# Forward product of a row block as one 512-column operand instead of two of 258, in a re-planned order

## The chip, the cores and the metric

The kernel runs on one core of a Trainium2 chip. The metric is the device time of one execution in microseconds (us); smaller is better. A profiled execution gives, beside it, the span from the first to the last instruction and what each engine did in it: PE (matrix products; PEld is its weight load), DVE and ACT (element-wise work, and copies between the matmul's result memory PSUM and the working memory SBUF), POOL and SP (here both used to issue DMA transfers).

## The reference

Two branches of the same size are mixed by a gate per row. Branch A filters its input in the frequency domain, branch B is a two-layer perceptron with GELU:

```python
# x, w_r, w_i: A_x (1, 2048, 512), (2048, 257); b: w1 (512, 1792), w2 (1792, 512)
X = rfft2(x)                       # over rows and columns
a = irfft2(X * (w_r + 1j * w_i), s=(2048, 512))
h = gelu(x @ w1 + b1)
b = h @ w2 + b2                    # both branches read A_x
g = sigmoid((x * gate_w).sum(-1))
out = g * a + (1 - g) * b
```

All of it is float32. The kernel keeps that precision by splitting each operand of a product into a high and a low part in a 12-bit-mantissa form (fp32r) and taking three matmuls, high times high, high times low and low times high.

## The kernel before

**Staging.** The 2048 rows are 16 residue classes j of 128 rows each (names like `xr4` or `py5` carry j). Five kinds of work share PE, and its results are named in the profile: `pd` and `py` are the forward transform of A, `pz` and `pa` its inverse, `ph` and `po` the two layers of B. The forward work of all blocks lies between about 10 and 120 us, and B's first half runs in between it; the inverse work and B's second half fill the rest.

**Forward transform of one block** (function `forward(j)`). DVE folds the block into even and odd parts (`eo`, `cl`), ACT and DVE split the result into `eoh` and `eol`. The first product `pd` (two results, c = 0 and 1, for the cosine and sine part along the 512 columns) takes for each c two matmuls of 260 columns and two of 130. ACT (L737) casts each `pd` to the high part `x..h`, DVE (L738, L739) forms the low part `x..l`, ACT copies four columns to `logit` for the gate (L740). The second product `py` transforms along the 128 rows, with a table `tf` of 64 cosine and 64 sine columns. A complex product needs cosine and sine exchanged for the sine part c = 1. The kernel before does that in the weights: ACT copies the first 64 table columns behind the last (L710), so that columns 0 to 127 serve c = 0 and columns 64 to 191 serve c = 1. Each c has its own PSUM bank `py`, filled by two high matmuls and one low matmul of 258 columns. ACT then copies the bank of c = 0 to `pys` (L757), DVE adds the bank of c = 1 (L758) and subtracts (L761); for 12 of the 16 blocks ACT moves the two 64-row halves of the difference to their places in `y` (L764), for the first four DVE subtracts straight into them (L767). All matmuls are issued by one helper, at L530.

**The head.** Before `forward` the inputs of blocks 0, 4, 8 and 12 (`xf`, `xr4`, `xr8`, `xr12`) are split for branch B too: ACT casts (`mxh`, L649), DVE subtracts (`mxl`, L650). The tile `ph` of the first layer needs the parts of two inputs for each half of its columns.

**What sets the order.** A planner (class `Graph`) is given every step with its engine, cost, latency, buffers and a due time, one entry of the table `RANKS` per step. It runs a list schedule over the steps: at each moment an engine takes the ready step with the earliest due time, and a buffer is given out when its last readers are done. The number of buffers of a kind that may be held at once is set by `slots` and `most` (`("pm", "py"): 3` means three banks). The order found is then emitted as it is, for all engines and for the DMA queues of SP and POOL. On the chip each engine takes its own list strictly in turn.

Of the kernel before, what the change touches and what calls it, by code (L numbers as in the profile page):

```python
# [11 lines left out]
F32 = mybir.dt.float32  # L12
# [5 lines left out]
P = 128  # L18
# [154 lines left out]
class Graph:  # L173
# [282 lines left out]
def tile_kernel(ctx: ExitStack, tc: tile.TileContext, xt, w1, w2, b1, b2, x0g, wf, wrev, out, consts):  # L456
# [13 lines left out]
             "so": 2, "ba": 2,  "pf": 2, "pm": 4, "ti": TI, "ring": RING, "hw": 8}  # L470

    whole = ("xr", "xm", "wra", "wrb", "e2", "z", "ttab", "xhl", "wa", "wb", "hid", "so", "ba", "ctab", "gb")
    most = {("pm", "ph"): 2, ("pm", "po"): 2, ("pm", "po0"): 1, ("pm", "py"): 3, ("t2k", "pq"): 2}
    g = Graph(slots, most)
    add = g.add

# [17 lines left out]
    def c_pe(n, k=1):  # L494
        return k * (n / 2400 + 0.0135) + 0.005
# [795 lines left out]
```

## Time and profile before

| | us |
|---|---|
| median of 3 runs | 372.97 (372.74 to 372.97) |
| span of the profiled execution | 370.8 |
| median less span (what lies around the span) | 2.17 |
| PE busy | 365.1 (98%) |
| PE's weight loads busy | 309.9 (84%) |
| DVE busy | 327.5 (88%) |
| ACT busy | 229.6 (62%) |
| POOL busy | 44.1 (12%) |

The profiled execution is given by its span alone; its own time is taken as the span with the 2.17 us around it. A matmul's recorded duration (0.39 us for 512 columns) is longer than the distance from its start to the next one's, since they are pipelined; sums over matmuls are therefore made from starts. A row of the timeline has the start, the time, the engine, the source line, the operation, the result and operands, the shape and how many were merged (x2), and in brackets an idle time ahead of it with what ended it. In a row of the chain of waits stand the start, the length and what the end of the program hung on at that time.

### The profile page before, as it was taken

The page shows a single profiled execution, that of the slowest core. Times are in us where ns is not written, and L with a number is a line of the kernel's source. Part 1 is how long each engine was busy: PE and PEld are TensorE (multiplying, and loading weights), DVE is VectorE, ACT ScalarE, POOL GpSimd, SP SyncE. Part 2 cuts the span into 40 slices and gives each one's busy share as a digit, 9 for nine tenths or more (in the row PEclk, how much of TensorE's full clock was granted, in tenths as well). Part 3 has the DMA queues.
Part 4 walks back from the last instruction along what each step waited for, and adds up shares of the span by engine and source line. Part 5 has one row for each costly group of instructions (what it writes and reads, how often), then busy time and mean ns, then how long its engine had stood idle before and what let it go on. Part 6 is the DMA issues. An engine that isn't in the chain of part 4 may idle for free.

```text
span 370.8 us, 5565 instructions
## 1 busy us (share of the span) xinstructions
PE 365.1 (98%) x1838; PEld 309.9 (84%) x1838; DVE 327.5 (88%) x691; ACT 229.6 (62%) x454; POOL 44.1 (12%) x54
## 2 busy tenths in 40 slices
PE   8999999999999999999999999999999999999995
PEld 6888888888888888888888888888888888888885
DVE  4999999999999789999999999588849696789996
ACT  5776587976678735375367213894697549457830
POOL 0000000000000002021032020001403222221031
PEclk9999999999999999999999999999999999999999
DMA  8962899425954216479289762318968999736268
GB/s 276 389 194 73 257 282 342 147 71 151 289 173 141 77 23 170 142 157 256 72 214 267 225 120 55 57 25 291 209 130 112 211 285 187 130 88 139 88 85 198
DMA packets 50868, 62.99 MB, mean 170 GB/s; under 512 B 4656, under 2 KB 31344, under 8 KB 50064
## 3 DMA queue, kind: packets, MB, share of 16 engines
q1 hardware_dynamic: 43496, 49.54, 41.3%
q0 software_dynamic: 7200, 12.85, 23.1%
q8 instruction: 14, 0.23, 0.2%
q10 hardware_dynamic: 144, 0.26, 0.2%
q14 instruction: 14, 0.11, 0.1%
HBM read 38.64 MB, written 23.73 MB: 168 GB/s over the span
## 4 chain that ended last, share of the span: by engine, by line
PE 95%; DVE 1%; DMA 1%; issue 0%; ACT 0%; SPq 0%; DVEq 0%
PE ph L530 41%; PE po L530 40%; PE pz L530 4%; PE pd L530 4%; PE py L530 3%; PE pa L530 3%; DMA xr<-in_xt 1%; DVE uv L1002 0%; DVE y L1021 0%; SPq L588 0%; DVE y L1024 0%; DVE mxl L650 0%; DVE o L1168 0%; ACT mxh L649 0%; ACT od L999 0%
## 5 line engine op out<-in xcount | busy, mean ns | idle before, releaser
L1106 ACT ACTIVATE ph<-ph,b1t 128x512 f32<-128x512 f32 x56 | 36.9, 659 | 41.5 <-PE ph L530 39.9
L949 ACT ACTIVATE sw<-y,al 64x512 f32<-64x512 f32 x32 | 23.0, 722 | 2.2 <-DVE y L812 1.6
L908 DVE TENSOR_TENSOR m<-y,wf 128x514 f32<-128x514 f32 x32 | 20.8, 689 | 0.2
L956 DVE SCALAR_TENSOR_TENSOR pq<-y,al,sw 128x256 f32<-128x256 f32 x32 | 14.4, 481 | 5.9 <-ACT sw L952 5.5
L521 POOL DMA_DIRECT2D bacc<-o x12 | 10.5, 877 | 73.2 <-ACT o L1155 60.2
L521 POOL DMA_DIRECT2D wa7l<-in_w x1 | 1.0, 1017 | 141.0 <-ACT wa7l L582 141.0
L1155 ACT ACTIVATE o<-po 128x512 f32<-128x512 f32 x12 | 7.1, 595 | 15.9 <-PE po L530 15.8
L1152 ACT ACTIVATE o<-po,b2t 128x512 f32<-128x512 f32 x16 | 10.7, 686 | 7.6 <-PE po L530 7.5
L1002 DVE TENSOR_TENSOR uv<-pa,od 128x512 f32<-128x512 f32 x16 | 10.6, 685 | 3.6 <-ACT od L999 3.5
L764 ACT ACTIVATE y<-pys 64x257 f32<-64x257 f32 x24 | 10.0, 418 | 5.2 <-DVE pys L761 4.8
L530 PE MATMUL pd<-cf,eoh 128*128 128x260 f32 x64 | 12.7, 285 | 0.0
L688 DVE TENSOR_TENSOR eo<-xr 128x256 f32<-128x256 f32 x30 | 12.0, 418 | 0.0
L530 PEld LDWEIGHTS pd<-cf,eoh 128*128 128x128 f32 x64 | 10.6, 189 | 1.5 <-issue 0.2
L999 ACT ACTIVATE od<-pa 128x512 f32<-128x512 f32 x8 | 4.8, 599 | 10.2 <-PE pa L530 9.9
L952 ACT ACTIVATE sw<-y 1x512 f32<-1x512 f32 x16 | 10.1, 629 | 0.4
L530 PE MATMUL pd<-cf,eol 128*128 128x130 f32 x64 | 10.3, 253 | 0.0
L702 DVE TENSOR_TENSOR xr<-eo 128x256 f32<-128x256 f32 x24 | 9.8, 418 | 0.1
L530 PEld LDWEIGHTS pd<-cf,eol 128*128 128x128 f32 x64 | 9.6, 189 | 0.1
L649 ACT ACTIVATE mxh<-xm 128x512 fp32r<-128x512 f32 x12 | 6.9, 623 | 3.7 <-PE ph L530 3.7
L650 DVE TENSOR_TENSOR mxl<-xm,mxh 128x512 fp32r<-128x512 f32 x12 | 7.8, 686 | 1.2 <-ACT mxh L649 1.2
L705 DVE TENSOR_TENSOR eol<-xr,eoh 128x512 fp32r<-128x512 f32 x12 | 8.3, 688 | 0.2
L1046 DVE SCALAR_TENSOR_TENSOR ba<-gb,ba 128x512 f32<-128x512 f32 x12 | 8.1, 685 | 0.3 <-DMA ba<-bacc 0.3
(713 smaller groups left out, 1353.6 us busy)
## 6 DMA issues: line engine op xcount, KB each, us to landing
wf<-in_wf SPq DMA_DIRECT2D x16, 257.0 KB, 4.9
bacc<-o SPq DMA_DIRECT2D x16, 256.0 KB, 3.3
xr<-in_xt SPq DMA_DIRECT2D x15, 256.0 KB, 3.5
war<-in_w SPq DMA_DIRECT2D x14, 256.0 KB, 3.5
wbr<-in_w SPq DMA_DIRECT2D x14, 256.0 KB, 3.5
xm<-in_xt SPq DMA_DIRECT2D x12, 256.0 KB, 4.3
bacc<-o POOLq DMA_DIRECT2D x12, 256.0 KB, 4.0
ba<-bacc SPq DMA_DIRECT2D x12, 256.0 KB, 3.2
```

What stands on the lines that cost most here:

```text
L521: return add("pool", kb / 150, 3.4, lambda: nc.gpsimd.dma_start(dst(), src(), accum_op=ALU.add), reads, writes, rank)
L530: pe.matmul(ps, w, x, start=start, stop=stop)
L688: v(lambda s=s, op=op: vec.tensor_tensor(eo.ap()[:, s], x.ap()[:, 0:2], x.ap()[:, 2:4], op=op), 256, [x], [(eo, s)], FEED)
L702: v(lambda k=k, op=op: vec.tensor_tensor(quarter(cl, k), eo.ap()[:, :, 0], eo.ap()[:, :, 1], op=op), 256, [eo], [(cl, k)] if j % 4 == 0 or ...
L764: a(lambda o=o, i=i: act.activation(Y[j].ap()[o:o + HP, 1], pys.ap()[i:i + HP, 1], AF.Copy), 257, [(pys, 1)], [(Y[j], 1 + k)], 0, more=0.1)
L908: v(lambda mk=mk, k=k, y=y, w=w: vec.tensor_tensor(mk.ap(), y.ap(), w.ap()[:, k:k + 1, :ND].to_broadcast([P, 2, ND]), op=ALU.mult), 514, [ ...
L949: a(lambda sw=sw, y=y, o=o, i=i: act.activation(sw.ap()[o:o + HP], y.ap()[i:i + HP, ::-1, :HD], AF.Copy, scale=al.ap()[i:i + HP, 0:1]), 51 ...
L952: a(lambda sw=sw, y=y, j=j: act.activation(sw.ap()[HP:HP + 1], y.ap()[HP:HP + 1, ::-1, :HD], AF.Copy, scale=math.cos(math.pi * j / NJ)), 5 ...
L956: v(lambda sw=sw, pq_=pq_, y=y, j=j, k=k, op=op: vec.scalar_tensor_tensor(pq_.ap()[:, k], y.ap()[:, k, :HD], al.ap()[:, 1 + j:2 + j], sw.a ...
L1002: v(lambda i=i, op=op: vec.tensor_tensor(uv.ap()[:, :, i], ps.ap()[:, 0], od.ap(), op=op), 512, [ps, od], [(uv, i)], 2)
L1106: a(lambda f=f, ps=ps: act.activation(ps.ap(), ps.ap(), AF.Gelu_apprx_tanh, bias=b1t.ap()[:, f:f + 1]), 600, [b1t], [ps], 0.9 if half else ...
L1152: a(lambda o=o, ps=ps, q=q: act.activation(o.ap(), ps.ap(), AF.Identity, scale=-1.0, bias=b2t.ap()[:, q:q + 1]), 600, [b2t, ps], [o])
```

## The change

Four things are changed.

1. The second product takes both parts side by side, `x..h` and `x..l` as 128 x 512 operands (256 columns of each c, where 258 were kept before), against the same table for both. So there is one bank `py` of 512 columns, filled by two high matmuls and one low one: 3 matmuls a block in place of 6.
2. The exchange of cosine and sine rows moves from the weights to the result. ACT copies the two 64-row halves of c = 1 crosswise to a buffer `sh` (L762; two such buffers, used in turn), leaving out one column, which is set to zero at the start. DVE adds (L764) and subtracts (L769, or L774 for the first four blocks) from it. Two copies of one column on ACT fill the last column of `y` (L765, L766). The table copy and `pys` before the sum are gone.
3. At most two `py` may be held (three before, of half the width). The planner's cost of a matmul gets a floor of 0.112 us, and the buffer `wf` shrinks from 288 to 272 columns.
4. All due times are replaced, so that every engine's order is new. They were found with a planning model in which transfers go by two DMA queues that alternate; nothing else in the code is different on that account, and transfers are issued from the same engines as before.

```diff
@@ -340,115 +340,116 @@
 RANKS = (
-    -149, 43, 217, 3, 143, 100, 150, 574, 1118, 447, 437, 885, 624, 1856, 1001, 866, 832, 912, 1753, 1799, 1869, 396,
...
+    5635, 2338, -1389, -2573, -2360, 2883, -642, -4771, -3130, 598, -859, -391, 836, 1229, 3747, 5202, 905, 2510, 1140,
...
@@ -470,7 +471,7 @@
-    most = {("pm", "ph"): 2, ("pm", "po"): 2, ("pm", "po0"): 1, ("pm", "py"): 3, ("t2k", "pq"): 2}
+    most = {("pm", "ph"): 2, ("pm", "po"): 2, ("pm", "po0"): 1, ("pm", "py"): 2, ("t2k", "pq"): 2}
...
     def c_pe(n, k=1):
-        return k * (n / 2400 + 0.0135) + 0.005
+        return k * max(n / 2400 + 0.0135, 0.112)
...
+    sh = [one(f"sh{k}", [P, ND], parts=3) for k in range(2)]
+    for b in sh:
+        add("vec", 0.1, 0.1, lambda b=b: vec.memset(b.ap()[:, P:P + 1], 0.0), [], [(b, 2)], 0.7)
...
-        t = buf("ttab", [P, 2, P + HP], F32R, f"tf{j}", parts=2)
-        dma(lambda: raw(t.ap()[:, :, :P], tf_d[j]), 128, [], [(t, 0)])
-        a(lambda: act.activation(t.ap()[:, :, P:], t.ap()[:, :, :HP], AF.Copy), P, [(t, 0)], [(t, 1)])
-
-        def ttab(k, c):
-            return t.ap()[:, k, c * HP:c * HP + P]
+        t = buf("ttab", [P, 2, P], F32R, f"tf{j}")
+        dma(lambda: raw(t.ap(), tf_d[j]), 128, [], [t])
...
         def body(c, k):
-            return some(c, [[511, 2], [1, P + 1]], 1 + k * NC)
+            return some(c, [[510 + c, 2], [1, P]], 2 + k * NC)
...
-        xh = buf("z", [P, 2, 512], F32R, f"x{j}h", parts=2)
-        xl = buf("z", [P, 2, 512], F32R, f"x{j}l", parts=2)
+        xh = buf("z", [P, 2, HD], F32R, f"x{j}h", parts=2)
+        xl = buf("z", [P, 2, HD], F32R, f"x{j}l", parts=2)
...
-        py = [buf("pm", [P, 512], F32, f"py{j}{c}", pool=pp, cls="py") for c in range(2)]
-        pys = t2k(f"pys{j}", cls="pys", parts=2)
-
-        def s_high(c):
+        py = buf("pm", [P, 2, HD], F32, f"py{j}", pool=pp, cls="py")
+        b = sh[NORD.index(j) % 2]
+
+        def flat(x):
+            return x.ap().rearrange("p a b -> p (a b)")
+
+        def s_high():
             for k in range(2):
-                mm(py[c].ap()[:, :NE], ttab(k, c), xh.ap()[:, c, :NE], k == 0, False)
-
-        def s_low(c):
-            mm(py[c].ap()[:, :NE], ttab(0, c), xl.ap()[:, c, :NE], False, True)
-
-        for c in range(2):
-            m(lambda c=c: s_high(c), NE, 2, [t, (xh, c)], [py[c]], 0)
-        for c in range(2):
-            m(lambda c=c: s_low(c), NE, 1, [t, (xl, c)], [py[c]], 0)
-        a(lambda: act.activation(pys.ap()[:, 0], py[0].ap()[:, 1:NE], AF.Copy), 257, [py[0]], [(pys, 0)], 0)
-        v(lambda: vec.tensor_tensor(Y[j].ap()[:, 0], py[1].ap()[:, 1:NE], pys.ap()[:, 0], op=ALU.add), 257, [py[1], (pys, 0)], [(Y[j], 0)], 0)
+                mm(flat(py), t.ap()[:, k], flat(xh), k == 0, False)
+
+        m(s_high, 512, 2, [t, xh], [py], 0)
+        m(lambda: mm(flat(py), t.ap()[:, 0], flat(xl), False, True), 512, 1, [t, xl], [py], 0)
         halves = ((0, HP), (HP, 0))
+
+        def around(x):
+            return bass.AP(tensor=x.tensor, offset=x.offset, ap=[list(x.ap[0]), [P + 1, 2], [1, P]])
+
+        for k, (o, i) in enumerate(halves):
+            a(lambda o=o, i=i: act.activation(around(b.ap()[o:o + HP]), py.ap()[i:i + HP, 1].rearrange("p (a b) -> p a b", a=2), AF.Copy), HD,
+              [py], [(b, k)], 0)
+        v(lambda: vec.tensor_tensor(Y[j].ap()[:, 0, :HD], py.ap()[:, 0], b.ap()[:, :HD], op=ALU.add), HD, [py, b], [(Y[j], 0)], 0)
+        a(lambda: act.activation(Y[j].ap()[:, 0, HD:], b.ap()[:, HD:], AF.Copy), 1, [(b, 0), (b, 1)], [(Y[j], 0)], 0)
+        a(lambda: act.activation(Y[j].ap()[:, 1, HD:], py.ap()[:, 1, HD - 1:], AF.Copy), 1, [py], [(Y[j], 1), (Y[j], 2)], 0)
         if j in BY_ACT:
-            v(lambda: vec.tensor_tensor(pys.ap()[:, 1], py[1].ap()[:, 1:NE], pys.ap()[:, 0], op=ALU.subtract), 257, [py[1], (pys, 0)],
-              [(pys, 1)], 0)
+            pys = buf("t2k", [P, HD], F32, f"pys{j}", cls="pys")
+            v(lambda: vec.tensor_tensor(pys.ap(), b.ap()[:, :HD], py.ap()[:, 0], op=ALU.subtract), HD, [py, b], [pys], 0)
...
```

What the new due times do is seen from the order of the instructions on an engine. On DVE, near the start, the four subtractions `mxl` of the head stand in the kernel before as follows (`xf0`, `xr4`, `xr8` and `xr12` are the inputs of blocks 0, 4, 8 and 12 and arrive in this order):

```order
L577 TENSOR_TENSOR wa0l_120<-war0_78,wa0h_108 128x512
L650 TENSOR_TENSOR mxl00_125<-xf0_76,mxh00_110 128x4x128
L650 TENSOR_TENSOR mxl00_125<-xr4_82,mxh00_110 128x4x128
L620 TENSOR_TENSOR gq_144<-gs_114 128x2
L650 TENSOR_TENSOR mxl00_125<-xr12_98,mxh00_110 128x4x128
L650 TENSOR_TENSOR mxl00_125<-xr8_96,mxh00_110 128x4x128
L577 TENSOR_TENSOR wa1l_160<-war1_100,wa1h_140 128x512
```

and in the changed kernel:

```order
L575 CAST wa0h_118<-war0_78 128x512
L655 TENSOR_TENSOR mxl00_123<-xf0_76,mxh00_114 128x4x128
L578 TENSOR_TENSOR wa0l_128<-war0_78,wa0h_118 128x512
L655 TENSOR_TENSOR mxl00_123<-xr4_86,mxh00_114 128x4x128
L655 TENSOR_TENSOR mxl00_123<-xr8_100,mxh00_114 128x4x128
L655 TENSOR_TENSOR mxl00_123<-xr12_102,mxh00_114 128x4x128
L622 TENSOR_TENSOR gs_112<-xf0_76 128x2
```

The subtraction for `xr8` has moved ahead of the one for `xr12`, and the weight's low part `wa0l` behind the subtraction for `xf0`.

On PE, in the middle of the forward work (blocks 5 and 9; `pd90` and `pd91` are block 9's first product for c = 0 and 1, `py50` and `py51` block 5's second), the kernel before has:

```order
L530 MATMUL pd90_788<-cf_132,eol9_724 128x130 x2
L530 MATMUL py50_804<-x5h_755,tf5_668 128x258 x2
L530 MATMUL py50_804<-x5l_763,tf5_668 128x258
L530 MATMUL pd91_812<-cf_132,eoh9_674 128x260 x2
L530 MATMUL pd91_812<-cf_132,eol9_724 128x130 x2
L530 MATMUL py51_819<-x5h_755,tf5_668 128x258 x2
L530 MATMUL py51_819<-x5l_763,tf5_668 128x258
L530 MATMUL py90_830<-x9h_810,tf9_707 128x258 x2
L530 MATMUL ph1_0_834<-mxh01_722,wa0h_108 128x512
```

and the changed one:

```order
L531 MATMUL py5_774<-x5h_715,tf5_644 128x512 x2
L531 MATMUL pd90_782<-cf_121,eoh9_698 128x260 x2
L531 MATMUL pd90_782<-cf_121,eol9_741 128x130 x2
L531 MATMUL pd91_790<-cf_121,eoh9_698 128x260 x2
L531 MATMUL pd91_790<-cf_121,eol9_741 128x130 x2
L531 MATMUL py5_774<-x5l_756,tf5_644 128x512
L531 MATMUL py9_818<-x9h_795,tf9_690 128x512 x2
L531 MATMUL ph1_0_825<-mxh01_679,wa0h_118 128x512
```

The high product of block 5 has moved ahead of block 9's `pd`, and between the last `pd91` and the second product of block 9 one matmul is left where three stood, of which the second product read one half of `x9h` and now reads both.

On ACT the casts of block 9 stand in the changed kernel with the copies that follow them (`sh1` is one of the two exchange buffers):

```order
L738 ACTIVATE x9h_795<-pd90_782 128x256
L741 ACTIVATE logit_355<-pd90_782 128x4
L738 ACTIVATE x9h_795<-pd91_790 128x256
L762 ACTIVATE sh1_80<-py5_774 64x2x128 x2
L741 ACTIVATE logit_355<-pd91_790 128x4
L766 ACTIVATE y_479<-py5_774 128x1
```

The casts come ahead of the row exchange of block 5, which was not there before.

More of the change, by code (lines that the diff above doesn't have):

```diff
@@ L724, in body @@
         def body(c, k):
-            return some(c, [[511, 2], [1, P + 1]], 1 + k * NC)
+            return some(c, [[510 + c, 2], [1, P]], 2 + k * NC)
         def two(t, c):
-            return t.ap()[:, c, :NE].rearrange("p (a b) -> p a b", a=2)
-        xh = buf("z", [P, 2, 512], F32R, f"x{j}h", parts=2)
-        xl = buf("z", [P, 2, 512], F32R, f"x{j}l", parts=2)
+            return t.ap()[:, c].rearrange("p (a b) -> p a b", a=2)
+        xh = buf("z", [P, 2, HD], F32R, f"x{j}h", parts=2)
+        xl = buf("z", [P, 2, HD], F32R, f"x{j}l", parts=2)
         n = j % 4 * 4 + j // 4
@@ L736, in forward @@
         for c in range(2):
-            a(lambda c=c: act.activation(two(xh, c), body(c, 0), AF.Copy), 258, [pd[c]], [(xh, c)], 0)
-            v(lambda c=c: vec.tensor_tensor(two(xl, c), body(c, 0), two(xh, c), op=ALU.subtract), 258, [pd[c], (xh, c)], [(xl, c)], 0)
-            v(lambda c=c: vec.tensor_tensor(two(xl, c), two(xl, c), body(c, 1), op=ALU.add), 258, [pd[c]], [(xl, c)], 0)
+            a(lambda c=c: act.activation(two(xh, c), body(c, 0), AF.Copy), HD, [pd[c]], [(xh, c)], 0)
+            v(lambda c=c: vec.tensor_tensor(two(xl, c), body(c, 0), two(xh, c), op=ALU.subtract), HD, [pd[c], (xh, c)], [(xl, c)], 0)
@@ L740, in forward @@
+            v(lambda c=c: vec.tensor_tensor(two(xl, c), two(xl, c), body(c, 1), op=ALU.add), HD, [pd[c]], [(xl, c)], 0)
             a(lambda c=c: act.activation(logit.ap()[:, n, c], some(c, [[641, 2], [NC, 2]], 0), AF.Copy), 4, [pd[c]],
               [(logit, 2 * n + c)], 0)
-        py = [buf("pm", [P, 512], F32, f"py{j}{c}", pool=pp, cls="py") for c in range(2)]
-        pys = t2k(f"pys{j}", cls="pys", parts=2)
-        def s_high(c):
-            for k in range(2):
-                mm(py[c].ap()[:, :NE], ttab(k, c), xh.ap()[:, c, :NE], k == 0, False)
@@ L763, in forward @@
             for k, (o, i) in enumerate(halves):
-                a(lambda o=o, i=i: act.activation(Y[j].ap()[o:o + HP, 1], pys.ap()[i:i + HP, 1], AF.Copy), 257, [(pys, 1)], [(Y[j], 1 + k)], 0, more=0.1)
+                a(lambda o=o, i=i: act.activation(Y[j].ap()[o:o + HP, 1, :HD], pys.ap()[i:i + HP], AF.Copy), HD, [pys], [(Y[j], 1 + k)], 0, more=0.1)
         else:
@@ L767, in forward @@
                 add("vec", 0.45, 0.1, lambda o=o, i=i: vec.tensor_tensor(
-                    Y[j].ap()[o:o + HP, 1], py[1].ap()[i:i + HP, 1:NE], pys.ap()[i:i + HP, 0], op=ALU.subtract),
-                    [(pys, 0), py[1]], [(Y[j], 1 + k)], 0)
+                    Y[j].ap()[o:o + HP, 1, :HD], b.ap()[i:i + HP, :HD], py.ap()[i:i + HP, 0], op=ALU.subtract),
+                    [b, py], [(Y[j], 1 + k)], 0)
         if j // 4 == 3:
@@ L897, in filt @@
             y = ys[q1]
-            w = buf("xr", [P, 2, 288], F32, f"wf{k2}")
+            w = buf("xr", [P, 2, 272], F32, f"wf{k2}")
             dma(lambda w=w, k2=k2: sp.dma_start(w.ap()[:, :, :ND], wf[k2]), 257, [], [w], 3)
```

217 rows, old and new, of the table RANKS are left out of this document.

## The prediction, made before the changed kernel was run

> **What bounds the kernel now.** I read the page's busy times first, then its chain of waits, then a table of stretches.
>
> ```profile
> PE 365.1 (98%) x1838; PEld 309.9 (84%) x1838; DVE 327.5 (88%) x691; ACT 229.6 (62%) x454; POOL 44.1 (12%) x54
> PE 95%; DVE 1%; DMA 1%; issue 0%; ACT 0%; SPq 0%; DVEq 0%
> 10.00:120.00 110.00, 110.00 (x590) 94.52 (x589) 107.11 (x252) 78.90 (x200) 0.00 (x0) 1.00 0.66 208
> ```
>
> The first row gives PE 365.1 of the 370.8 us of the span; the second says that 95% of the chain that ended last is PE. The third row is the stretch from 10 to 120 us, in which all 16 row blocks pass the changed code (columns: PE, PEld, DVE, ACT, POOL, granted clock, DMA share, GB/s). PE is never idle there and runs at full clock. DVE works 107.11 of 110 us, so it has 2.9 us to spare; ACT has 31. So the kernel ends when PE has issued its matmuls, and three things can move the time: the sum of the matmul slots, a stall of PE, and the parts before the first and after the last matmul. The span of the profiled execution is 370.8; the median of the runs is 372.97, so 2.17 us lie around it. I sum on the span and add 2.17.
>
> **Part 1: 96 matmuls of 258 columns become 48 of 512.** What counts is not a matmul's duration, which overlaps the next, but the distance from start to start. The chain of waits gives the time in which each product is what PE advances by, and the timeline shows single slots:
>
> ```profile
> by line: PE po L530 39.8%; PE ph L530 33.1%; PE pd L530 14.2%; PE py L530 13.3%
> 46.84 0.39 PE L530 MATMUL po<-g_6h,wb6h 128*128 128x512 f32 x1
> 47.08 0.39 PE L530 MATMUL po<-g_6l,wb6h 128*128 128x512 f32 x1
> 47.30 0.39 PE L530 MATMUL po<-g_6h,wb6l 128*128 128x512 f32 x1
> 47.53 0.28 PE L530 MATMUL py<-x12l,tf 128*128 128x258 f32 x1
> 47.65 0.41 PE L530 MATMUL py<-x12h,tf 128*128 128x258 f32 x2
> 47.90 0.28 PE L530 MATMUL py<-x12l,tf 128*128 128x258 f32 x1
> 48.02 0.40 PE L530 MATMUL py<-x1h,tf 128*128 128x258 f32 x2
> 48.25 0.41 PE L530 MATMUL pd<-cf,eoh 128*128 128x260 f32 x2
> 343.12 2.72 PE ph L530 x12
> ```
>
> The first row is the chain from 28 to 118 us: py is 13.3% of 90 us, 11.97 us for 96 matmuls. Of the singles, 47.65 to 48.02 holds three py matmuls in 0.37, 47.53 to 47.65 one in 0.12: 0.72 to 0.74 for the six of a block. The 512-column slot is 2.72/12 = 0.227 undisturbed and (47.53 − 46.84)/3 = 0.230 here, so three take 0.68 to 0.69. The difference is 0.03 to 0.06 a block, 0.5 to 1.0 in all; by the chain's total it is 11.97 − 48 × 0.2275 = 1.05. That total also holds what a matmul loses behind a pair of 128x130 ones (part 4's rows: 55.70 to 55.99 is 0.29 for a pair of py where 48.02 to 48.25 is 0.23), a loss that the next matmul pays whatever it is, and the pd pairs stay. So I take the lower part, **−0.68**, with 1.05 as the far end. The near end is a product that pays by columns alone: 6 × 258 − 3 × 512 = 12 columns a block at 0.227/512 us each, 0.09 in all.
>
> The Trainium skill, "TensorE: Matmul & The Clock Gate", section "Back-to-back issue gap", puts a warm matmul at N ÷ 2.4 GHz plus about 2.5 ns, which is 110.0 and 215.8 ns here and would make this term only −0.2. The slots above are longer, 120 and 227 ns, about 13 ns over the columns, and the measurement decides; but by that rule the change would be worth next to nothing, and rival D carries it.
>
> **Part 2: rows exchanged on ScalarE.** Per block go the copy of the table (L710) and the copy pys (L757); two 64-row copies and two of one element come.
>
> ```profile
> L757 ACT ACTIVATE pys<-py x16: 370/387/389, 32.4 to 115.6; 128x257 f32<-128x257 f32 x16
> L710 ACT ACTIVATE tf<-tf x16: 297/312/342, 9.5 to 105.4; 128x128 fp32r<-128x128 f32 x16
> L740 ACT ACTIVATE logit<-pd x32: 152/174/205, 27.9 to 107.3; 128x4 f32<-128x4 f32 x32
> L764 ACT ACTIVATE y<-pys 64x257 f32<-64x257 f32 x24 | 10.0, 418 | 5.2 <-DVE pys L761 4.8
> ```
>
> No row shows a 64-row copy out of PSUM; 387 ns (128 rows from PSUM) and 418 ns (64 rows, also moved across partitions) lie on both sides, and I take 418. The one-element copies I price like the smallest row, 174 ns. 2 × 0.418 + 2 × 0.174 − 0.387 − 0.312 = +0.49 a block, +7.8 us on ACT (+7.3 with 387), under its 31 idle us in that stretch: nothing on the end unless a PE wait ends on ACT. DVE keeps its number of operations (691 rows, 693 after; two small memsets ahead of the first data), 2 columns fewer in each. Cost 0; if ACT's cover were gone at every block it would be 0.49 each, which is rival C.
>
> **Part 3: the new order at the head.** These rows of the timeline (the DMA queues' and some others are left out) are the split of the first block's four inputs:
>
> ```profile
> 5.39 0.69 DVE L650 TENSOR_TENSOR mxl<-xf,mxh 128x512 fp32r<-128x512 f32 x1
> 6.00 0.68 DVE L650 TENSOR_TENSOR mxl<-xr,mxh 128x512 fp32r<-128x512 f32 x1
> 6.73 0.54 PEld L530 LDWEIGHTS ph<-mxl,wa0h 128*128 128x128 f32 x4
> 6.89 0.63 ACT L649 ACTIVATE mxh<-xr 128x512 fp32r<-128x512 f32 x1 [0.58 <-DMA xr<-in_xt]
> 7.55 1.29 DVE L650 TENSOR_TENSOR mxl<-xr,mxh 128x512 fp32r<-128x512 f32 x2 [0.80 <-ACT mxh L649]
> 7.57 0.53 PEld L530 LDWEIGHTS ph<-mxh,wa0h 128*128 128x128 f32 x4 [0.30 <-ACT mxh L649]
> 8.90 0.54 PEld L530 LDWEIGHTS ph<-mxl,wa0h 128*128 128x128 f32 x4 [0.32 <-DVE mxl L650]
> 9.48 0.40 PE L530 MATMUL ph<-mxh,wa1h 128*128 128x512 f32 x1
> ```
>
> and, from the chain of waits, four matmuls of 256 columns that nothing holds up:
>
> ```profile
> 359.94 0.47 PE pa L530 x4
> ```
>
> DVE sits idle 0.80 us up to 7.55, because in its queue the subtraction for the late input (xr12, whose cast ends at 7.52) stands ahead of the one for xr8, which has long been there. Then it does both, 1.29 us, and PE waits for the second at 8.90. In the new order xr8 comes first. By DVE's spacing of 0.61 I place them: xf 5.17, wa0l 5.78, xr4 6.39, xr8 7.00, xr12 7.61 to 8.30. The tile's last four low products (256 columns each) begin at 8.90 and the next tile at 9.48, 0.58 later where 0.47 would do: a stall costs PE about 0.1 more than its wait. In the new order PE takes its first low products at 7.11 in place of 6.73 and needs 0.47 + 0.10, to 7.68. The cast of xr12 is in by then, the low parts of xr8 and xr12 are before their turn at 8.62, and three groups of 0.47 bring the next tile to 9.09 in place of 9.48: **−0.39**. Bounds: 0, if the first half, now 0.38 later, is later still and pushes the second, to −0.49, if it costs no restart.
>
> **Part 4: one product of two halves needs both halves.** In the new order, PE does both pd products of block 9, then the low product of block 5 (one matmul, 0.23), then py9. In the trace these are the same steps in the old order:
>
> ```profile
> 54.70 0.34 PE L530 MATMUL pd<-cf,eol 128*128 128x130 f32 x2
> 55.15 0.38 ACT L737 ACTIVATE x9h<-pd 128x258 fp32r<-128x258 f32 x1
> 55.28 0.40 PE L530 MATMUL pd<-cf,eoh 128*128 128x260 f32 x2
> 55.52 0.34 PE L530 MATMUL pd<-cf,eol 128*128 128x130 f32 x2
> 55.70 0.46 PE L530 MATMUL py<-x5h,tf 128*128 128x258 f32 x2
> 55.76 0.68 ACT L1152 ACTIVATE o<-po,b2t 128x512 f32<-128x512 f32 x1
> 55.99 0.28 PE L530 MATMUL py<-x5l,tf 128*128 128x258 f32 x1
> 56.11 0.41 PE L530 MATMUL py<-x9h,tf 128*128 128x258 f32 x2
> 56.34 0.39 ACT L737 ACTIVATE x9h<-pd 128x258 fp32r<-128x258 f32 x1
> ```
>
> Before, py of x9's first half started at 56.11, 0.96 after its cast began, and the second half's cast at 56.34 hurt nobody: its product came later. Now, from the start of the last pd pair: the pair ends at +0.34, ACT casts from +0.38 to +0.77, py9 can start at +0.82. PE is free at 0.18 (55.52 to 55.70) + 0.05 (the loss behind a pair) + 0.23 = +0.46. So PE waits 0.36, with part 3's 0.1 to get going: **+0.46**. Bounds: 0, if PE gets there late for another reason, to 0.36 + 0.68 + 0.1 = 1.14, if an eviction like the one at 55.76 stands ahead of the cast. The ph matmuls behind wait for DVE's subtractions of the next column block, which this pause covers.
>
> **Part 5: the end.** The queues' rows there:
>
> ```profile
> 361.77 0.61 ACT od L999
> 362.40 1.30 DVE uv L1002 x2
> 363.72 1.29 DVE y L1021 x2
> 366.22 0.66 DVE o L1168 x2
> ```
>
> After PE's last pa the end hangs on DVE alone. The new order has the same operations there, with one output sum between other two: 0, ±0.3.
>
> Sum: 370.8 − 0.68 − 0.39 + 0.46 = 370.2, plus 2.17: **372.35 us**.
>
> **The rivals.**
>
> B, the pause at py9 does not appear, and the sum of slots falls by the chain's total: −1.05 − 0.39 = −1.44 with both, −1.07 with the first alone; about **371.7**. For it: in all of 10 to 120 us PE has no idle time now, although casts end as tightly elsewhere. Against it: the arithmetic of part 4 has only rows in it.
>
> C, slower: the exchange holds the one py bank. Its place is the path py → ACT → DVE. Before, half a product lay in each of two banks, one read by ACT (387 ns), one by DVE. Now the sum on DVE waits for two ACT copies, 2 × 0.418 in place of 0.387, so each bank comes free 0.45 later, and only two py are allowed where there were three of half the width. DVE has 2.9 us of slack over 110, 0.18 a block. If a quarter of the 0.45, 0.11, and 0.05 to restart reach PE in each block, that is 16 × 0.16 = +2.5, less 0.6: **374.9**; with half of the blocks 373.6. It decides from 1.4 us of such waits on, 0.09 a block. For it: DVE at 97%. Against it: DVE's work is not more, and ACT's idle time is.
> The Trainium skill, "PSUM — Partial Sum Buffer", holds that two engines must not access one bank on the same partitions at once; that rule makes ACT's and DVE's reads of the joined bank take turns, as rival C has it. No run here shows the price yet.
>
> D, one of the savings is not there: slots go by columns (−0.09 in place of −0.68, which the 13 ns of part 1 speak against), or the head's 0.39 is eaten by its first half. Then 372.97 − 0.09 − 0.39 + 0.46 = 372.95 or 372.74: about **372.85**.
>
> **How the numbers follow.** My forecast 0.45, B 0.24, C 0.13, D 0.18. A measurement of this kernel tells 0.2%, 0.75 us, from no change: faster is under 372.22, slower over 373.72. The forecast's own range is 371.9 to 372.9 (0.45 from part 4's and 0.3 from part 5's bounds), of which 0.16 lies under 372.22; with nearly all of B (0.23) and a little of D, faster gets 0.40. Slower gets C's 0.11 and 0.02 of the forecast with part 4's far end: 0.13. The rest, 0.47, is no change that can be measured. The range of 371.4 to 374.0 holds all but the far ends of B and most of C.
>
> **What would show it.** Part 1: py in the chain of waits with 48 matmuls and about 11 us; near 11.9 it is wrong. Part 3: no PE wait at the last low products near 8.62, and the first matmul of the second ph tile at 9.1 in place of 9.48. Part 4: an idle time of PE (or its weight loads) ahead of py<-x9h, ended by the cast, 0.3 to 0.4 long. Rival C: idle PE rows ahead of py or pd, released by ACT or DVE, over 0.09 a block. I am wrong if PE's busy time is not about 0.7 lower, or if stalls appear at more places than py9.

## The result and the profile after

The changed kernel takes 375.45 us (median of 5 runs, 375.07 to 375.75), the kernel before 372.94 (5 runs, 372.16 to 372.97): a ratio of 1.0072, with a 95% interval of 1.0060 to 1.0085. It is slower by 2.5 us; the forecast was 372.35, and 375.45 lies outside its range. The profiled execution has a span of 374.0, 3.2 more than before; it was the longest of the five. Its time is 1.75 over its span, and in every run on record the time is 1.7 to 1.9 over the span; so the profiled execution of the kernel before, taken with 2.17 ahead of the prediction, was some 0.4 faster than its median. That is why the spans differ by 3.2 and the medians by 2.5.

The page's busy times and chain of waits, and the stretch from 10 to 120 us (columns as in the prediction), of the changed kernel:

```profile
PE 366.8 (98%) x1790; PEld 307.5 (82%) x1790; DVE 327.9 (88%) x693; ACT 237.1 (63%) x486; POOL 44.1 (12%) x54
PE 94%; DVE 3%; ACT 2%; issue 0%
10.00:120.00 110.00, 108.58 (x531) 89.89 (x530) 103.85 (x247) 84.40 (x227) 0.00 (x0) 1.00 0.66 205
```

DVE's work is the same (327.9 against 327.5), ACT has 7.5 more (7.8 was priced). But between 10 and 120 us PE is now idle for 1.42 us where it was never idle, and DVE for 6.15 where it was 2.89. The list of what PE's weight loads waited for shows the places; its rows give the total, the number and the longest. Before, from 10 to 130 us, these three are all:

```profile
PEld py L530 <- ACT logit L740: 0.2, 1, 0.2
PEld py L530 <- ACT pys L757: 0.2, 1, 0.2
PEld pd L530 <- issue: 0.2, 1, 0.2
```

After, the first rows of the same list:

```profile
PEld pd L531 <- DVE x2l L740: 0.9, 1, 0.9
PEld pd L531 <- ACT x8h L738: 0.6, 1, 0.6
PEld py L531 <- ACT x9h L738: 0.5, 1, 0.5
```

I add up what every matmul's start is late against the regular distance for its shape (0.227 us for 512 columns, 0.120 for 256 to 260, 0.060 inside a pair of 130 columns and 0.1115 from its second matmul to the next, which itself takes 0.05 more; all are medians of the two traces). From 9.5 us on that is 4.78 us after and 1.31 before. The places of over 0.06 us make 3.4 of the 4.78, and 0.14 of the 1.31. These are the main ones after:

| start, us | what PE began there | lost, us |
|---|---|---|
| 37.7 | pd of block 8, second half | 0.65 |
| 41.8, 42.1 | py of block 8 | 0.17 |
| 55.6, 55.8 | pd of block 9 | 0.24 |
| 57.2, 57.5 | py of block 9 (the one predicted) | 0.36 + 0.11 |
| 71.8, 72.3 | py of block 2 and the next | 0.19 |
| 74.1 | pd of block 6, second half | 0.90 |
| 110.2, 110.5 | py of block 11 | 0.22 |
| 118.8 to 126.2 | ph, behind g_1l and g_2l | 0.37 |

The account of the span, against before: waits +3.47; the head +0.02 (the second ph tile starts at 9.50, before at 9.48); the end +0.31 (from the last eviction od on ACT to the last DVE operation 5.91 for 5.78, the last transfer 0.18 more). Together +3.80; the span grew by 3.20, so the shorter slots gave back 0.60. The slots themselves say the same: 96 of 0.120 are 11.52, 48 of 0.227 are 10.90, 0.62 less.

**How the largest wait came about.** The timeline of the changed kernel, ACT, DVE and PE ahead of 74.1:

```profile
69.11 0.66 ACT L1113 ACTIVATE ph<-ph,b1t 128x512 f32<-128x512 f32 x1
69.25 0.69 DVE L578 TENSOR_TENSOR g_1l<-ph,g_1h 128x512 fp32r<-128x512 f32 x1 [0.38 <-ACT g_1h L577]
69.78 0.77 ACT L762 ACTIVATE sh<-py 64x256 f32<-64x256 f32 x2
70.58 0.17 ACT L766 ACTIVATE y<-py 128x1 f32<-128x1 f32 x1
...
70.78 0.42 DVE L769 TENSOR_TENSOR pys<-sh,py 128x256 f32<-128x256 f32 x1 [0.51 <-ACT y L766]
...
72.04 0.42 DVE L740 TENSOR_TENSOR x2l<-x2l,pd 128x256 fp32r<-128x256 f32 x1 [0.16 <-ACT logit L741]
...
73.65 0.41 DVE L740 TENSOR_TENSOR x2l<-x2l,pd 128x256 fp32r<-128x256 f32 x1
74.12 0.51 PE L531 MATMUL pd<-cf,eoh 128*128 128x260 f32 x2 [0.74 <-DVE x2l L740]
```

DVE has already waited 0.38 us for ACT's cast of `g_1h`, which belongs to B. It then stands still for 0.51 us until ACT, after an activation of B and the two row copies, has made its one-column copy from the same bank. The row copies end at 70.55, and `pys` needs them in any case; so 0.3 of the 0.51 is the length of ACT's list, and 0.2 the copy behind them, whose result `pys` doesn't use. DVE loses another 0.16 to ACT's copy for the gate, which reads the bank pd. DVE's list is full, so the loss stays, and PE, which needs the bank that x2l empties, waits at 74.12.

At 37.7 it is the same with the gate's copies alone:

```profile
34.57 0.43 DVE L739 TENSOR_TENSOR x4l<-pd,x4h 128x256 fp32r<-128x256 f32 x1
...
35.03 0.24 ACT L741 ACTIVATE logit<-pd 128x4 f32<-128x4 f32 x2 [0.22 <-DVE x4l L739]
35.30 0.42 DVE L739 TENSOR_TENSOR x4l<-pd,x4h 128x256 fp32r<-128x256 f32 x1 [0.30 <-ACT logit L741]
...
37.12 0.42 DVE L740 TENSOR_TENSOR x4l<-x4l,pd 128x256 fp32r<-128x256 f32 x1
37.23 0.38 ACT L738 ACTIVATE x8h<-pd 128x256 fp32r<-128x256 f32 x1 [1.36 <-PE pd L531]
...
37.68 0.48 PE L531 MATMUL pd<-cf,eoh 128*128 128x260 f32 x2 [0.48 <-ACT x8h L738]
```

ACT waits for DVE to be done with a bank, then DVE for ACT with the next: 0.30 us of DVE. PE starts when DVE's last step on x4l has ended at 37.54; the profile names ACT's x8h, which ended last but reads the other pd buffer.

### The profile page after: what moved, and what is told of

It is laid out like the page before. It is cut to its first block, busy times and chain, and to the rows that moved or that the text cites. A ratio compares the mean times of both kernels' runs of the same rounds, so it can differ in the third digit from the quotient of the medians.

```text
span 374.0 us, 5524 instructions
## 1 busy us (share of the span) xinstructions
PE 366.8 (98%) x1790; PEld 307.5 (82%) x1790; DVE 327.9 (88%) x693; ACT 237.1 (63%) x486; POOL 44.1 (12%) x54
## 4 chain that ended last, share of the span: by engine, by line
PE 94%; DVE 3%; ACT 2%; issue 0%
PE ph L531 40%; PE po L531 40%; PE pz L531 4%; PE pd L531 3%; PE py L531 3%; PE pa L531 3%; PE none L531 1%; DVE o L1180 0%; DVE y L1031 0%; DVE uv L1009 0%; ACT ph L1113 0%; DVE xr L707 0%; ACT y L771 0%; ACT x9h L738 0%; ACT sh L762 0%
## 5 line engine op out<-in xcount | busy, mean ns | idle before, releaser
L762 ACT ACTIVATE sh<-py 64x256 f32<-64x256 f32 x32 | 12.2, 380 | 3.7 <-PE py L531 3.0
L771 ACT ACTIVATE y<-pys 64x256 f32<-64x256 f32 x24 | 9.9, 417 | 2.4 <-DVE pys L769 1.9
L522 POOL DMA_DIRECT2D out<-ba x8 | 7.0, 872 | 16.8 <-DVE ba L1053 9.4
```

What stands on the lines that cost most here:

```text
L522: return add("pool", kb / 150, 3.4, lambda: nc.gpsimd.dma_start(dst(), src(), accum_op=ALU.add), reads, writes, rank)
L762: a(lambda o=o, i=i: act.activation(around(b.ap()[o:o + HP]), py.ap()[i:i + HP, 1].rearrange("p (a b) -> p a b", a=2), AF.Copy), HD, [py], ...
L771: a(lambda o=o, i=i: act.activation(Y[j].ap()[o:o + HP, 1, :HD], pys.ap()[i:i + HP], AF.Copy), HD, [pys], [(Y[j], 1 + k)], 0, more=0.1)
```

## The experiments

The theories: **T1**, ACT and DVE read one PSUM bank in turn, and the turns cost DVE time that it has not got. **T2**, the new due times leave no slack, whoever reads what. **T3**, the longer way through ACT costs by its length. "Before" was run beside each group, with medians of 372.60 to 372.83; the changed kernel was not run again, so gains are given against its 375.45.

The turns of T1 are waits for semaphores, in the order of the program. The planner doesn't know them: in `Graph.add` a read depends on the last write, and a write on the reads before it, but never a read on another read. No run here was made to let the two engines read one bank at once; what is priced below is the order.

### Taking the turns away, same order

```diff
-act.activation(Y[j].ap()[:, 1, HD:], py.ap()[:, 1, HD - 1:], AF.Copy)
+act.activation(Y[j].ap()[:, 1, HD:], cft.ap()[:, 0, 0, 0:1].bitcast(F32), AF.Copy)
```

> The changed kernel, every engine's order unchanged, but the one-column copy on ScalarE reads the table cf in place of the bank py (the instruction stays, the last column of y is left out of the computation). Theory T1 (the joined bank is read by ACT and DVE in turn; the DVE idle time of 0.51 us ahead of pys at 70.3, ended by this copy, makes the PE wait of 0.9 at 74): that wait goes, 1.0 us off, 374.4. Theory T2 (the new due times leave too little slack between ACT, DVE and PE, whoever reads what): at most 0.3 off, 375.1 or more.

And, for the second, the gate's copies as well:

```diff
-act.activation(logit.ap()[:, n, c], some(c, [[641, 2], [NC, 2]], 0), AF.Copy)
+act.activation(logit.ap()[:, n, c], cft.ap()[:, 0, 0, 0:4].rearrange("p (a b) -> p a b", a=2).bitcast(F32), AF.Copy)
```

> As the run before, and the 4-column copies for the gate read the table cf too, in place of pd (the gate's sum is left out of the computation). T1: the 0.30 us of DVE ahead of x4l at 35.3 go, with them the PE wait of 0.65 at 37.7: together 1.8 off, 373.6. T2: at most 0.5 off, 374.9 or more.

These two leave the last column of y, and the second also the gate's sum, out of the result. Measured: 381.87 (381.50 to 382.19) and 380.19 (379.15 to 381.10), slower than either theory had. The edit had a side effect of its own: cf was now read until 118 us, so that the load of ci into its place stood in SP's queue until 118.18 (111.30 in the changed kernel), with the gate's transfers behind it, and PE waited at 124.9. Up to there the traces can be compared. The same ph matmul that starts at 118.78 in the changed kernel starts at 118.01 in the first of the two; the wait at 74 is 0.68 in place of 0.90, that at 37.7 is 0.46 in place of 0.65. So T1's number for the first missed: 0.22 of the wait at 74 went, not all of it. DVE still waits there, now for the row copies:

```profile
69.82 0.42 DVE L769 TENSOR_TENSOR pys<-sh,py 128x256 f32<-128x256 f32 x1 [0.31 <-ACT sh L762]
```

In the second run the wait at 74 is gone and that at 37.7 is down to 0.14. The second was repeated with another source:

```diff
-cft.ap()[:, 0, 0, 0:4]
+b1t.ap()[:, 0:4]
-cft.ap()[:, 0, 0, 0:1]
+b1t.ap()[:, 0:1]
```

> As e2_no_turn_py_pd (changed kernel, ACT's 1-column and 4-column copies read no PSUM bank; the last column of y and the gate's sum are left out of the computation), but reading b1t, which stays in memory for the whole run, in place of the table cf, whose longer life held up the load that replaces it. T1 (turns on the banks): the waits of PE at 37.7 and 74.1 are gone and 2.0 us with them, 373.4. T2 (due times without slack): 374.9 or more. The wait ahead of py9 of 0.36 stays in both.

Measured: 373.27 (372.76 to 373.91), 2.2 under the changed kernel. T1's number was 373.4; T2 is out as the only cause. Without the turns ACT's own list runs earlier too, so the 2.2 is what the turns cost together with what they delay. The wait at py9 is 0.36 and 0.11, unchanged.

### Moving the copies: fewer turns in the whole kernel, more turns in the one before

```diff
     order = g.schedule()
+    for cast, gate_copy in MOVE:
+        order.remove(gate_copy)
+        order.insert(order.index(cast) + 1, gate_copy)
+    for row_copies, column_copy in AHEAD_OF:
+        order.remove(column_copy)
+        order.insert(min(order.index(x) for x in row_copies), column_copy)
```

> The changed kernel, whole, with ACT's order alone altered: each 4-column copy for the gate directly behind the cast that reads the same bank, the 1-column copy of py directly ahead of the two row copies, so that ACT is done with a bank before DVE turns to it (waits of these copies on DVE: 8 before, 0 now). T1: 1.2 to 2.0 off, 373.4 to 374.2. T2: at most 0.5 off. A third way: ACT's casts now come 0.1 to 0.2 later each, and the time doesn't fall.

Measured: 373.76 (373.23 to 374.45), 1.7 less, inside T1's interval; nothing but ACT's list differs, and nothing is left out of the result. The wait at 74.1 is gone, that at 37.7 is 0.32. Now the other way, in the kernel before:

```diff
     order = g.schedule()
+    for subtraction, gate_copy in MOVE:
+        order.remove(gate_copy)
+        order.insert(order.index(subtraction) + 1, gate_copy)
```

> The kernel before with ACT's order altered the other way: each 4-column copy behind DVE's subtraction from the same bank, so that ACT and DVE take turns at 30 of the 32 banks pd in place of 3. Nothing else. T1: each turn costs DVE or ACT 0.1 to 0.3; DVE has 2.9 us to spare between 10 and 120, so 30 turns bring PE waits of 1 to 5 us, 374 to 378. T2: under 0.5 more, 373.4 at most.

Measured: 375.71 (375.08 to 375.99), 3.0 more than before, a ratio of 1.0075 (1.0053 to 1.0097). Its list of DVE's waits begins:

```profile
DVE x4l L740 <- ACT x4h L739: 0.5, 1, 0.5
DVE x10l L741 <- ACT logit L742: 0.5, 2, 0.2
DVE x1l L741 <- ACT logit L742: 0.5, 2, 0.2
DVE x13l L741 <- ACT logit L742: 0.5, 1, 0.5
```

Where the kernel before loses no more than 0.2 at a time, this has eleven rows ended by the gate's copies. The turns alone, without the new product and without its due times, make a loss of the size of the change's. That the 30 turns also make ACT wait for DVE, and its next cast come later, belongs to it.

### The length of ACT's work

For the second of the two halves alone (half of the exchange is left out of the result, and the two buffers `sh` are zeroed whole at the start):

```diff
-act.activation(around(b.ap()[o:o + HP]), py.ap()[i:i + HP, 1].rearrange("p (a b) -> p a b", a=2), AF.Copy)
+act.activation(b.ap()[o:o + HP, 0:1], py.ap()[i:i + HP, 1, 0:1], AF.Copy)
```

> The changed kernel, same order, with the second of the two row copies of each block cut to one column (its other rows of the buffer are zero, so half of the exchange is left out of the computation). ACT is 0.21 shorter per block there, and DVE's sum can start that much earlier. T3 (the longer way through ACT costs by its length): 0.8 to 1.2 off, 374.3 to 374.7. T1: at most 0.4 off, 375.0 or more.

Measured: 373.49 (373.25 to 374.50), 2.0 less, or 1.7 by the ratios to the kernel before (1.0027 for 1.0072). That is more than T3 had (0.8 to 1.2) and far more than T1 allowed: the length counts too. The waits at 37.7 (0.43) and 74.1 (0.72) are still there, those behind 75 us are gone. So I asked whether the two act on the same slack:

> f3_copies_moved with the shortened second row copy of f6_short_row_copy (half of the exchange is left out of the computation). If the turns on the banks and the length of the row copies each cost PE waits of their own, both gains add: 375.45 - 1.7 - 2.0 = 371.8. If both only draw on the same slack between ACT and DVE, so that either of them ends most of the waits, the second brings little: 373.0 to 373.6.

(both edits above together). Measured: 372.52 (372.16 to 372.87), 1.2 under the one and 1.0 under the other; alone they were worth 1.7 and 2.0. They share some 0.7 (0.4 by the ratios) and add for the rest: neither is the whole cause. DVE still stands idle for 3.55 us between 10 and 120 us there (2.89 before), and with half of the exchange left out the time is that of the kernel before, 372.60 (ratio 0.9994, 0.9986 to 1.0003).

Then ACT's load by itself, in the kernel before:

```diff
-act.activation(pys.ap()[:, 0], py[0].ap()[:, 1:NE], AF.Copy)
+act.activation(pys.ap()[:, 0], py[0].ap()[:, 1:NE], AF.Copy), act.activation(spare.ap()[:HP], pys.ap()[:HP, 0, :200], AF.Copy)
```

> The kernel before with one more copy on ACT per block, right behind pys: 64 rows of 200 columns from pys to a buffer that nobody reads, some 0.35 us, 5.6 us in all, about what the changed kernel adds to ACT between 10 and 120 us (5.5). No other engine waits for it. If ACT's 31 idle us hide it, as the prediction had it: 372.4 to 373.0. If ACT's queue is tight at the casts that DVE and PE wait for, whatever its idle time in sum: 373.6 to 375.

Measured: 374.42 (374.31 to 375.45), +1.6, ratio 1.0047 (1.0032 to 1.0063). The group of the added copy (lowest, median and highest time in ns), and where PE's loads wait in this kernel:

```profile
L758 ACT ACTIVATE spare<-pys x16: 370/371/372, 32.6 to 117.5; 64x200 bf16<-64x200 f32 x16
PEld pd L530 <- issue: 0.7, 3, 0.3
PEld py L530 <- ACT tf L711: 0.6, 1, 0.6
PEld py L530 <- ACT pys L758: 0.5, 2, 0.3
PEld ph L530 <- ACT pys L758: 0.2, 1, 0.2
```

16 times 0.371 is 5.9 us, which nobody reads, put on an engine that was idle for 31 of 110 us: PE waits for what stands behind it, and 1.6 us of the 5.9 reach the end. With the copy ahead of pys in place of behind it:

```diff
-act.activation(pys.ap()[:, 0], py[0].ap()[:, 1:NE], AF.Copy)
+act.activation(spare.ap()[:HP], py[0].ap()[:HP, 1:201], AF.Copy), act.activation(pys.ap()[:, 0], py[0].ap()[:, 1:NE], AF.Copy)
```

> As h1_before_act_busier, but the copy stands ahead of pys and reads the same bank py, so that pys, and DVE's sum behind it, come 0.35 later, as the second row copy makes them in the changed kernel. If only ACT's load counts: as h1. If the longer path from py through ACT to DVE counts beside it: 0.5 to 1.5 more than h1. If neither: 372.4 to 373.0.

Measured: 373.90 (373.34 to 375.08), +1.1, ratio 1.0033 (1.0020 to 1.0046), not more than the copy behind it, though pys and the sum are 0.33 later in each block (its median is 0.331; read from PSUM it is shorter). So of T3 the queue on ACT is what shows; that the path py, ACT, DVE is longer adds nothing that can be seen here, where the py banks are three.

### The due times

```diff
-    5635, 2338, -1389, -2573, -2360, 2883, -642, -4771, -3130, 598, -859, -391, 836, 1229, 3747, 5202, 905, 2510, 1140,
+    -149, 43, 217, 3, 143, 100, 150, 574, 1118, 447, 437, 885, 624, 1856, 1001, 866, 832, 912, 1753, 1799, 1869, 396,
...
```

> The changed product (parts 1 to 3 of the change) under the due times of the kernel before: the joined high product gets the later of the two old due times, the row copies that of pys, the one-column copies that of the sum plus 0.5 us. T1 and a theory T3 (the longer way through ACT is what costs, in any order): PE waits at several blocks stay, 374 to 375.5. T2: PE keeps the 0.7 us of shorter slots and loses little of it, 372.3 to 373.0.

Measured: 381.28 (380.71 to 383.50), outside all of them. From 10 to 130 us its largest PE waits are mostly at other work:

```profile
PEld ph L530 <- DVE g_2l L577: 2.4, 1, 2.4
PEld pd L530 <- issue: 1.7, 5, 0.5
PEld py L530 <- DVE g_6l L577: 0.9, 1, 0.9
PEld pd L530 <- DVE x5l L742: 0.8, 1, 0.8
```

Due times found for one set of steps did not fit this other one. This run can't tell T2 from T3 and settles nothing but that the old due times can't be kept.

### The head

```diff
     order = g.schedule()
+    order.remove(low_xr8)
+    order.insert(order.index(low_xr12), low_xr8)
```

> The kernel before with one step moved: the subtraction for xr8 ahead of the one for xr12 on DVE, as in the changed kernel. If the prediction's step was right, the second ph tile starts 0.39 earlier than at 9.48 and the time falls by 0.3 to 0.4, to 372.6. If a late fast clock eats it (in the changed kernel's trace the 11 warm-up matmuls took 5.06 us in place of 4.54), the time depends on that and the gain is 0 to 0.4 from run to run.

Measured: 372.48 (372.03 to 373.48) against 372.71, a ratio of 0.9994 (0.9982 to 1.0007): a gain can't be told from none. PE's first rows in the kernel before and in the changed one (row `none` is the 11 warm-up matmuls), and of this run the chain of waits at its head:

```profile
1.06 4.54 PE L530 MATMUL none<-zero 128*128 128x512 f32 x11 [1.06 <-DVE zero L593]
```
```profile
1.05 5.06 PE L531 MATMUL none<-zero 128*128 128x512 f32 x11 [1.05 <-DVE sh L595]
6.09 1.08 PE L531 MATMUL ph<-mxh,wa0h 128*128 128x256 f32 x4
9.50 0.40 PE L531 MATMUL ph<-mxh,wa1h 128*128 128x512 f32 x1
```
```profile
0.73 4.30 DMA xf<-in_x0g
5.06 1.16 ACT mxh L649 x2
6.26 3.92 PE ph L530 x27
```

In the profile of the kernel before the first ph matmul started at 5.68. In the traces of the changed kernel and of the twelve experiments it starts between 5.78 and 6.26, because xf landed later (at 5.03 in the last fence; before, ACT had begun on it at 4.48) or because the warm-up matmuls took 5.06 us, and not 4.54. The wait at the last low products, 0.32 in the profile before, is there in three of the five traces with the old order on DVE (0.22 to 0.32) and in none of the nine with xr8 first. But the second ph tile begins no earlier for it: at 9.24 to 9.48 in the five, at 9.20 to 9.67 in the nine. The step is worth nothing that these show.

### A version with the remaining waits moved

In short, with names in place of the search for each step:

```diff
+    put(step("vec", "x4l", 3), y_of_block_0, behind=False)
+    put(step("vec", "x5l", 2), step("vec", "x5l", 1), behind=False)
+    put(step("vec", "eol13", 0), step("vec", "x5l", 3))
+    put(step("sp", "xr10", 0), step("vec", "eol13", 0))
+    put(po_g6, step("pe", "pd91", 1))
+    put(step("act", "o0_03", 0), gate_copy_of_pd91)
+    put(step("vec", "g2_2l", 0), y_ahead_of_it, behind=False)
```

> f3_copies_moved, whole, with five more steps moved, each at one of the PE waits that are left in it: x4l's last step ahead of a subtraction of y (wait of 0.32 at 37.2), x5l's steps ahead of eol of block 13 (0.24 at 55.0), three po matmuls from ahead of py5 to behind pd91, with their eviction behind the casts of x9h (0.36 and 0.11 at py9), and g_2l ahead of a sum of y (0.21 at 124.1). If the waits are what is left of the loss and the 0.7 us of shorter slots are real, 1.0 to 1.3 off: 372.4 to 372.8, no slower than the kernel before. If moving them opens as many waits elsewhere, 373.3 to 374.

The transfer of xr10 is moved with eol13, whose input it overwrites. Measured: 373.67 (373.36 to 374.52), no better than the 373.76 it started from. Its PE list shows the second case, waits that moved:

```profile
PEld ph L534 <- ACT o L1165: 0.5, 1, 0.5
PEld py L534 <- ACT x5h L743: 0.4, 1, 0.4
PEld pd L534 <- ACT logit L746: 0.4, 2, 0.2
```

The wait at py9 is gone and the one behind it, for the eviction that had been put off, took 0.26 + 0.11. No version tried was measurably faster than the kernel before.

### What ties the runs together

| kernel | us | DVE idle, 10 to 120 us | ACT busy there |
|---|---|---|---|
| before | 372.94 | 2.89 | 78.90 |
| before, xr8 first | 372.48 | 2.88 | 78.95 |
| before, gate's copies taking turns | 375.71 | 5.89 | 77.86 |
| before, ACT busier, behind pys | 374.42 | 4.66 | 81.59 |
| before, ACT busier, ahead of pys | 373.90 | 4.20 | 80.27 |
| changed | 375.45 | 6.15 | 84.40 |
| changed, copies moved | 373.76 | 4.73 | 85.92 |
| changed, copies and waits moved | 373.67 | 4.77 | 86.04 |
| changed, no turns | 373.27 | 4.17 | 87.25 |
| changed, short row copy | 373.49 | 4.18 | 83.30 |
| changed, both | 372.52 | 3.55 | 84.19 |

The time goes with DVE's idle time in this stretch, not with ACT's busy time. At about the same idle time the changed kernels are lower than the others, as their shorter slots have it (375.45 at 6.15 and 375.71 at 5.89; 373.27 at 4.17 and 373.90 at 4.20). (Idle is 110 less the busy time of DVE in that stretch; the two runs that read cf and the one with the old due times, which lose much behind 120 us, are left out.) The table alone names no cause: DVE has the same work in both kernels, so whatever costs time gives it idle time. What raises it is shown by the edits, each of which left the rest of the order as it was: turns on a bank, put in and taken out, and a longer ACT queue ahead of what DVE needs, lengthened and shortened.

## Why the prediction was wrong, by its own steps

- **What bounds the kernel**: right that only slots, stalls of PE and the two ends count. The slack was looked for in the wrong place: 31 idle us of ACT were taken as cover, and the 2.89 of DVE only as a point of rival C.
- **Part 1** (−0.68): right, with 0.60 in the account. Its own sign, a busy time of PE 0.7 lower, could not show it: the busy time rose from 365.1 to 366.8, because a matmul's recorded time is longer than its slot, and a wait shorter than the difference counts as busy. The figure of the Trainium skill ("TensorE: Matmul & The Clock Gate", section "Back-to-back issue gap"), by which it would have been −0.2, is not borne out.
- **Part 2** (0): the step that failed. "under its 31 idle us in that stretch: nothing on the end unless a PE wait ends on ACT" put the cost at 0, and the overlap that it counted on was not there. ACT's length was priced about right (+7.8, measured +7.5; a row copy 0.38 in place of 0.418, a one-column copy 0.17 and 0.20; its "+7.3 with 387" takes the lower price for one of the two row copies, with both it is +6.8). But an engine that is idle 28% of a stretch can still be late at the moments that count, through DVE too, where no PE wait names ACT: the largest wait of PE ends on DVE's x2l. Adding 16 copies of 0.37 us to ACT alone cost 1.6, and cutting the second row copy gave back 1.7 to 2.0. The turns were not in part 2 at all; they stood in rival C.
- **Part 3** (−0.39): the mechanism was right, the wait of DVE and that of PE at the last low products went. The size was not: the first ph matmul starts up to 0.58 later in other executions than in the profile that the sum went by, two of the five traces with the old order don't have the wait that was to go, and the tile behind it starts no earlier in the new order; the account has +0.02.
- **Part 4** (+0.46): right in place and size, 0.36 and 0.11, the same in every trace with that order. It said nothing of the 0.24 at 55.6, where the pd of block 9 waited for x5l, and which also made the pause come later.
- **Part 5** (0 ± 0.3): +0.31 with the last transfer, at the edge of its range.
- **Rival C**, with 0.13, was nearest in kind: reads of a joined bank in turn, and DVE without slack. It put the price at 373.6 to 374.9, spread over the blocks, by each py bank coming free later. The measured waits are few and large, and where the list of waits of PE's weight loads names an engine at a py, it is ACT with a cast (x9h and x2h), not a reader of an earlier py; that only two py may be held was not tested by itself. About half of what the turns cost up to 90 us comes from the gate's copies on pd, which the new order sets apart from their casts and which the rival didn't name: there PE is late by 3.16 in the changed kernel, by 2.29 without the turns on py (the first run with cf) and by 1.47 without those on pd either (the run with b1t). Its counter-argument, that ACT has idle time, is the step of part 2 again. The rule of the Trainium skill beside it ("PSUM — Partial Sum Buffer", section "PSUM bank collisions raise a hardware error", that two engines must not be on one bank at once) has a price here: moving ACT's small copies so that turns vanish gave 1.7 us, putting 30 turns into the kernel before took 3.0.

What stays open: how much of the changed kernel's loss is the order rather than the product. The waits at py9, at pd of block 9 and behind the evictions are of the order, as far as the traces tell; with all copies moved 1.1 us above before remain, and a run with the old due times didn't settle it.

## What to carry to other kernels

Look for slack on the engine that feeds the bottleneck, in the stretch in question, and at the moments that count, not in the sum: DVE at 97% had no time for a wait of 0.3, and an idle share of 28% on ACT didn't cover 0.37 a block. When two engines read one PSUM bank, let the first be done with all its reads before the second begins; joining two banks into one brings such turns along with the saving. A planner that doesn't know reads of one bank as an order can put a cheap copy where it costs, as this one did.

## What was not expected of the hardware

Behind a long pause PE was slow for a while. After the wait of 6.14 us in the first experiment (rows of PE in its timeline), the 512-column slots are 0.43 us, and only from 134.82 on 0.23 to 0.25:

```profile
131.25 0.79 PE L531 MATMUL ph<-mxh,wa4h 128*128 128x512 f32 x1 [6.14 <-DVE g_2l L578]
131.84 0.63 PE L531 MATMUL ph<-mxl,wa4h 128*128 128x512 f32 x1
...
134.82 0.41 PE L531 MATMUL ph<-mxh,wa4l 128*128 128x512 f32 x1
135.07 0.40 PE L531 MATMUL ph<-mxh,wa4h 128*128 128x512 f32 x1
```

The granted clock (third figure from the end, in stretches of its trace) says the same, 0.50 and then 1.00:

```profile
132.00:133.00 1.00, 1.00 (x4) 0.81 (x3) 1.00 (x3) 1.00 (x2) 0.00 (x0) 0.50 0.28 77
135.00:136.00 1.00, 1.00 (x7) 0.79 (x6) 0.00 (x0) 0.04 (x1) 0.00 (x0) 1.00 0.00 0
```

That adds some 1.7 us to the pause. The run with the old due times has it too, behind a wait of 2.0 us that ends at 128.70: 0.43 us a slot from 129.5 to 132.9, and a granted clock of 0.50 between 130 and 132. None of the waits of under 1 us in the table of lost time is followed by such slots. The Trainium skill, "TensorE: Matmul & The Clock Gate", section "Back-to-back issue gap", puts a cold matmul at N ÷ 1.2 GHz, an estimate of 426.7 ns for 512 columns, which agrees with the 0.43. The 11 warm-up matmuls at the start, ahead of which PE had done nothing, took from 4.11 to 5.06 us in different executions, where 11 slots of 0.227 would be 2.5; and where they took 5.06 the first ph matmuls were slow too. The granted clock reads 1.00 there, so that only the slots show it.
